# Three weight transfers asked for at other places of the start, one of them by another queue

## The chip, the cores and the metric

The kernel runs on one core of a Trainium2 chip. A core has five engines with an instruction stream each: TensorE (PE, matmuls and transposes), VectorE (DVE), ScalarE (ACT), GpSimd (POOL) and SyncE (SP), which only asks for DMA transfers. SP and ACT each have a DMA queue, and both queues are served by the same 16 DMA engines; in the profile, q1 is SP's queue and q10 is ACT's. The metric is the device time of one execution in microseconds, as the median of several executions; lower is better.

## The reference

Two stages follow each other. The first is an mLSTM cell with 4 batches, 8 heads, 768 steps and a head dimension of 40:

```python
for t in range(S):
    m_new = np.maximum(f_gate[:, :, t] + m, i_gate[:, :, t])
    f_stab, i_stab = np.exp(f_gate[:, :, t] + m - m_new), np.exp(i_gate[:, :, t] - m_new)
    C = f_stab * C + i_stab * outer(v_t, k_t)      # one 40x40 state for each batch and head
    n = f_stab * n + i_stab * k_t
    y[:, :, t] = sigmoid(o_gate_t) * (C @ q_t) / maximum(abs(n @ q_t), 1)
```

The second is a SwiGLU block on the 3072 tokens of width 320 that come out of it, with a hidden width of 1536:

```python
g = x @ w_gate
out = (g * sigmoid(g) * (x @ w_val)) @ w_out
```

The inputs of the first stage are float32. The three weight matrices arrive as float64, so the kernel reads them as pairs of 32-bit words and converts them to float32 itself.

## The kernel before

**Tiling.** The sequence is cut into six groups of 128 steps. For each group the kernel computes the cell's output in a chunked form (scores inside a chunk, a running state between chunks), turns it into `xT`, the transposed input of the second stage, and then runs the second stage on the group's 512 tokens. The hidden width is cut into 12 blocks of 128, m = 0 to 11. For group g, `hidden(g, m)` makes 20 matmuls (five chunks of 64 features, each for the gate and the value weights, and each matmul of float32 stands twice in the profile) into two PSUM banks, then ACT takes SiLU of the gate bank and DVE multiplies it with the value bank into `h_sb`. There are four such banks (`gen`), so block m needs the banks of block m - 2 back. After the blocks, `project` multiplies `h_sb` with the output weights `wo_sb`.

**Order.** The order of the instructions of each engine is the order in which the program text calls them (`manual_schedule`); no planner moves anything. Waits between engines come from the data that instructions share. A DMA transfer also takes one of eight DMA semaphores in turn and waits until the transfer that had it before has landed.

**Weights.** A piece is one or more blocks of weights, and is loaded by `piece_load(p)`: pieces 0 and 1 hold one block each (block 0, block 1), pieces 2 to 6 hold two blocks each (2 and 3, 4 and 5, 6 and 7, 8 and 9, 10 and 11), and pieces 7 to 9 hold the output weights. Pieces 0 to 6 come in two halves: the gate half, which goes to partitions 0 to 63, and the value half, which goes to partitions 64 to 127. A half is 320 KB for pieces 0 and 1 and 640 KB for the others. "The third piece" below is piece 2, "the fourth" piece 3, "the fifth" piece 4. The raw words land in the two buffers `raw` in turn, except for piece 2, which lands in a part of `h_sb` that is not used yet, and piece 3, which lands in `wo_sb`, also not used yet. The gate half is asked for by SP. Who asks for the value half is in one line:

```python
queues = (nc.sync, nc.scalar if p < 5 else nc.sync)
```

A block is then converted in three steps, `convert(j)`: `scale(j)` on ACT (`top`, then `low`, L190 and L192), `join(j)` on DVE (L199, L200) and `rounded(j)` on POOL or DVE (L207). In the first group the conversions of later blocks stand inside `hidden(0, m)`, ahead of the SiLU of that block: `hidden(0, 0)` converts block 2, `hidden(0, 1)` block 3, and so on.

**The start.** Everything around the change stands in the stretch before the first `hidden`: ACT loads the sigmoid's table and takes `sig(0)` and `sig(1)` of the output gates `o_sb` (heads 0 to 15 and 16 to 31, L463), then copies `xT`, scales block 0, copies `xT` again, scales block 1, takes the exp of `step1` (L609) and scales block 2. SP's stream asks in this stretch for the gate halves, then for the first group's `M_sb` to be written to `M_dram`, and then for what the second group (n = 1) needs: k and q (`load_all`, L117), piece 6, the attention weights `w_sb` from `M_dram` (`weights_load`, L447), v, the output weights and the output gates. `weights_sub` (L451) is the first to read `w_sb`, on DVE, and stands between the products of blocks 6 and 7 of the first group.

Of the kernel before, what the change touches and what calls it, by code (L numbers as in the profile page):

```python
# [12 lines left out]
U32 = mybir.dt.uint32  # L13
# [11 lines left out]
def kernel(  # L25
# [18 lines left out]
    nc = tc.nc  # L44
# [12 lines left out]
    NKC = DM // HP  # L57
    UH = BH // 2
    UA = UH // 2
    NH = NFC + 1  # L60
# [25 lines left out]
    def heads(P):  # L86
        return slice(P * UH, (P + 1) * UH)
# [13 lines left out]
    wo_sb = const.tile([128, NFC, DM], F32)  # L101
    h_sb = const.tile([128, NH, TW], F32)
# [34 lines left out]
    raws = {}  # L137
    PIECES = [("gv", 0, 1), ("gv", 1, 1)] + [("gv", m, 2) for m in range(2, NFC, 2)] + [("o", m, 4) for m in range(0, NFC, 4)]

    def piece_load(p, home=None):  # L140
        kind, m, n = PIECES[p]
        if kind == "gv":
            a, d = NKC, n * 128
            src = [(slice(i * HP, (i + 1) * HP), w[:, m * 128:(m + n) * 128].rearrange("(c p) f -> p c f", p=HP))
                   for i, w in enumerate((moe_w_gate, moe_w_val))]
            queues = (nc.sync, nc.scalar if p < 5 else nc.sync)
        else:
            a, d = n, DM
            src = [(slice(0, 128), moe_w_out[m * 128:(m + n) * 128].rearrange("(a p) d -> p a d", p=128))]
            queues = (nc.sync,)  # L150
        if src[0][1].dtype == F32:
            for r, w in src:
                if kind == "o":
                    nc.sync.dma_start(out=wo_sb[r, m:m + n, :], in_=w)
                else:
                    for x in range(n):
                        nc.sync.dma_start(out=wgv_sb[r, m + x], in_=w[:, :, ts(x, 128)])
            return
        if home is None:
            raw = conv.tile([128, 4 * NKC * 128], U32, name="raw")  # L160
        else:
            raw = home.rearrange("p a t -> p (a t)").bitcast(U32)
        raw = raw[:, 0:2 * a * d]
        for (r, w), queue in zip(src, queues):
            queue.dma_start(out=raw[r].rearrange("p (a d) -> p a d", a=a), in_=w.bitcast(U32))
        words = raw.rearrange("p (a d two) -> p a d two", two=2, a=a)
        raws[p] = (words[:, :, :, 0], words[:, :, :, 1])
        split(p)
# [4 lines left out]
    def split(p):  # L173
        if p in raws:
            lo, hi = raws.pop(p)
            kind, m, n = PIECES[p]
            if kind == "gv":
                for c in range(n):
                    r = slice(c * 128, (c + 1) * 128)
                    blocks[m + c] = (lo[:, :, r], hi[:, :, r], wgv_sb[:, m + c])  # L180
            else:
                for c in range(0, n, 2):
                    blocks[NFC + (m + c) // 2] = (lo[:, c:c + 2], hi[:, c:c + 2], wo_sb[:, m + c:m + c + 2, :])

    def scale(j):
        if j in blocks:
            lo, hi, dst = blocks[j]
            a, d = hi.shape[1], hi.shape[2]
            top = conv.tile([128, NKC * 128], F32, name="top", bufs=1).rearrange("p (a d) -> p a d", a=a)
            nc.scalar.mul(top, hi.bitcast(F32), 2.0 ** -112)  # L190
            low = conv.tile([128, NKC * 128], I32, name="low").rearrange("p (a d) -> p a d", a=a)
            nc.scalar.mul(low, lo, 2.0 ** -29)  # L192
            blocks[j] = (low, top.bitcast(U32), dst)

    def join(j):
        if j in blocks:
            lo, top, dst = blocks[j]
            both = dst.bitcast(U32)
            nc.vector.tensor_scalar(both, top, scalar1=3, scalar2=None, op0=ALU.logical_shift_left)  # L199
            nc.vector.scalar_tensor_tensor(both, in0=top, scalar=0x80000000, in1=both, op0=ALU.bitwise_and,  # L200
                                           op1=ALU.bitwise_or)
            blocks[j] = (lo, dst.bitcast(I32))

    def rounded(j, eng=None):
        if j in blocks:
            lo, dst = blocks.pop(j)
            (eng or nc.gpsimd).tensor_tensor(dst, dst, lo, op=ALU.add)  # L207

    def convert(j, eng=None):
        scale(j)  # L210
        join(j)
        rounded(j, eng)
# [34 lines left out]
    for u in range(B):  # L247
        r = slice(u * BH, (u + 1) * BH)
# [34 lines left out]
    def late_decay():  # L283
        nc.vector.tensor_add(m_in[:, 0:1], M0[0:BH, end].unsqueeze(1), f0[0:BH, end].unsqueeze(1))
        nc.vector.tensor_add(m_in[:, 1:], M_sb[:, 0:NL - 1, last], f_sb[:, 0:NL - 1, last])
        nc.vector.tensor_sub(step1, m_in.to_broadcast([BH, NL, SUB]), M_sb)
# [175 lines left out]
    def sig(P):  # L462
        nc.scalar.activation(o_sb[:, heads(P)], o_sb[:, heads(P)], AF.Sigmoid)  # L463


    def burn(n, tag="cell"):
        t = bank("burn", tag)
        for _ in range(n):
            nc.tensor.matmul(t, lhsT=junk[:, 0:128], rhs=junk, start=True, stop=True)
# [62 lines left out]
    def first_x(u):  # L532
        y = first_y.pop(u)
        den = work.tile([128, UH, 1], F32, name="den")[:, 0:H]
        nc.vector.tensor_scalar(den, y[:, :, D:], scalar1=1.0, scalar2=None, op0=ALU.max)
        nc.vector.scalar_tensor_tensor(den, in0=y[:, :, D:], scalar=-1.0, in1=den, op0=ALU.mult, op1=ALU.max)
        nc.vector.reciprocal(den, den)
        nc.vector.tensor_tensor(x_sb[:, u, 0:DM].rearrange("p (h d) -> p h d", d=D), y[:, :, 0:D],
                                den.to_broadcast([128, H, D]), op=ALU.mult)
# [39 lines left out]
    first_turn(1, q_sb, qT, (A, V))  # L579
    load(o_sb, o_gate, 0, 1)  # L580
    piece_load(0)
    piece_load(1)
    late_maxima()
    first_own(1)
    first_values(1)
    first_scores(1)
    first_x(1)
    sig(0)
    sig(1)
    piece_load(2, h_sb[:, NH - NKC:])  # L590
    piece_load(3, wo_sb)
    burn(3)
    first_own(2)
    first_own(3)
# [11 lines left out]
    first_state(0, A)  # L606
    late_decay()
    convert(1)
    nc.scalar.activation(step1, step1, AF.Exp)  # L609
    piece_load(5)  # L610
    nc.sync.dma_start(out=M_dram, in_=flat(M_sb))
# [234 lines left out]
```

## Time and profile before

| what | value |
|---|---|
| time, median of 3 runs | 555.15 us (554.77 to 555.56) |
| profiled execution: time | 555.16 us |
| profiled execution: span, first to last instruction | 553.0 us |
| TensorE busy | 546.4 us, 99% of the span |
| ScalarE busy | 134.7 us, 24% |
| VectorE busy | 234.4 us, 42% |
| q1 (SP): packets, MB | 222036, 42.11 |
| q10 (ACT): packets, MB | 1908, 2.85 |
| granted clock of TensorE | 1.000 |

The time of an execution is some 2 us longer than the span of its instructions. In the timeline, a row has its start in us, its busy time, the engine, the line, the operation, the output and the inputs, and in brackets how long the engine was idle before it and what ended that wait. Rows of SPq and ACTq are the instructions by which SP and ACT ask for transfers, and their time is that of the asking. In the chain of waits, a row with DMA runs from the asking to the landing.

### The profile page before, as it was taken

How to read it: one execution, taken by the hardware profiler on the slowest of the kernel's cores; microseconds unless marked ns; L12 is line 12 of the kernel's file. 1: busy time of each engine (PE TensorE's matmuls, PEld its weight loads, DVE VectorE, ACT ScalarE, POOL GpSimd, SP SyncE). 2: the span in 40 equal slices, each digit the busy share in tenths (PEclk: the TensorE clock that was granted, in tenths of full speed). 3: DMA queues.
4: the chain of work that ended last, by engine and by line, in shares of the span. 5: the costliest groups of instructions: out<-in, count | busy, mean ns of one | idle time of the engine just before them, and what ended most of it. 6: DMA issues, size and time to landing. Idle time of an engine off the chain costs nothing.

```text
span 553.0 us, 11595 instructions
## 1 busy us (share of the span) xinstructions
PE 546.4 (99%) x4992; PEld 312.9 (57%) x4992; DVE 234.4 (42%) x394; ACT 134.7 (24%) x202; POOL 106.6 (19%) x97
## 2 busy tenths in 40 slices
PE   8999999999999999999999999999999999999997
PEld 4955546675545575544576455466455567444475
DVE  5956687962156332445521445531426621011100
ACT  4366564443101033110124101005110100111100
POOL 2314355574011151011133001114001200000000
PEclk9999999999999999999999999999999999999999
DMA  9999996798631763660464451395000131000000
GB/s 125 177 280 187 192 274 115 155 111 125 68 49 17 108 109 83 71 76 5 82 127 104 53 68 27 49 149 107 13 1 2 29 62 43 12 1 0 2 24 24
DMA packets 223994, 45.69 MB, mean 83 GB/s; under 512 B 214504, under 2 KB 219112, under 8 KB 223944
## 3 DMA queue, kind: packets, MB, share of 16 engines
q1 hardware_dynamic: 222036, 42.11, 46.7%
q10 hardware_dynamic: 1908, 2.85, 2.0%
q8 instruction: 39, 0.64, 0.5%
q14 instruction: 11, 0.09, 0.1%
HBM read 35.68 MB, written 4.01 MB: 72 GB/s over the span
## 4 chain that ended last, share of the span: by engine, by line
PE 92%; DMA 4%; SPq 3%; POOL 0%; DVE 0%; ACT 0%; issue 0%; ACTq 0%; POOLq 0%
PE gv_ps L648 55%; PE o_ps L664 24%; PE o_ps L671 5%; SPq L117 3%; DMA h_sb<-in_moe_w_val_dram 2%; PE inter L377 2%; PE sp L331 2%; PE intra L382 2%; DMA o_sb<-in_o_gate_dram 2%; PE add L353 1%; PE tp_kq L296 0%; POOL wgv_sb L207 0%; PE tp_x L439 0%; DVE wgv_sb L200 0%; ACT top L190 0%
## 5 line engine op out<-in xcount | busy, mean ns | idle before, releaser
L648 PE MATMUL gv_ps<-xT,wgv_sb 64*128 64x512 f32 x1440 | 317.3, 593 | 1.6 <-POOL wgv_sb L207 1.1
L648 PEld LDWEIGHTS gv_ps<-xT,wgv_sb 64*128 64x128 f32 x1440 | 139.1, 187 | 159.4 <-issue 154.6
L654 DVE TENSOR_TENSOR h_sb<-sg,gv_ps 128x512 f32<-128x512 f32 x72 | 49.5, 687 | 214.5 <-ACT sg L653 214.4
L664 PE MATMUL o_ps<-wo_sb,h_sb 128*128 128x320 f32 x480 | 130.5, 433 | 0.0
L664 PEld LDWEIGHTS o_ps<-wo_sb,h_sb 128*128 128x128 f32 x480 | 90.8, 190 | 41.0 <-issue 3.8
L653 ACT ACTIVATE sg<-gv_ps 128x512 f32<-128x512 f32 x72 | 43.0, 597 | 268.6 <-PE gv_ps L648 268.5
L362 POOL TENSOR_TENSOR C<-C,dec 128x328 f32<-128x328 f32 x20 | 14.5, 735 | 137.7 <-DVE C L369 137.6
L456 POOL TENSOR_SCALAR_AFFINE_SELECT w_sb<-w_sb 64x1024 f32<-64x1024 f32 x20 | 27.8, 1388 | 60.2 <-DVE w_sb L451 59.3
L658 ACT COPY z_sb<-o_ps 128x320 f32<-128x320 f32 x24 | 10.0, 422 | 94.7 <-PE o_ps L664 90.9
L403 POOL TENSOR_TENSOR o_sb<-o_sb,y_sb 128x640 f32<-128x640 f32 x10 | 14.3, 1428 | 79.2 <-DVE y_sb L394 79.1
L671 PE MATMUL o_ps<-wo_sb,h_sb 128*128 128x320 f32 x96 | 26.9, 437 | 0.0
L451 DVE TENSOR_TENSOR w_sb<-g_T,w_sb 128x1024 f32<-128x1024 f32 x10 | 13.2, 1355 | 27.6 <-DMA w_sb<-M_dram 27.6
L426 DVE STREAM_TRANSPOSE xT<-x_sq 128x640 f32<-128x640 f32 x16 | 12.5, 822 | 23.7 <-DMA x_sq<-x_sb 23.7
L671 PEld LDWEIGHTS o_ps<-wo_sb,h_sb 128*128 128x128 f32 x96 | 17.9, 190 | 7.2
L394 DVE TENSOR_TENSOR y_sb<-y_sb,intra 64x328 f32<-64x328 f32 x40 | 19.7, 493 | 0.8 <-PE intra L382 0.2
L369 DVE TENSOR_TENSOR C<-C,add 40x328 f32<-40x328 f32 (+1 forms) x36 | 17.7, 493 | 1.3 <-PE add L353 0.4
L207 POOL TENSOR_TENSOR wgv_sb<-wgv_sb,low 128x640 int32<-128x640 int32 x8 | 12.3, 1541 | 23.7 <-DVE wgv_sb L200 21.9
L377 PEld LDWEIGHTS inter<-C,qT 64*64 64x64 f32 x640 | 10.2, 134 | 7.3 <-issue 6.1
L341 POOL TENSOR_TENSOR vw_sb<-v_sb,w_sb 128x656 f32<-128x656 f32 x10 | 12.8, 1303 | 0.4
L338 DVE TENSOR_TENSOR w_sb<-sp,w_sb 128x512 f32<-128x512 f32 x20 | 12.7, 682 | 0.0
L460 ACT ACTIVATE w_sb<-w_sb 128x1024 f32<-128x1024 f32 x10 | 10.6, 1058 | 8.8 <-POOL w_sb L456 8.8
L397 DVE TENSOR_SCALAR den<-den 128x16 f32<-128x16 f32 x10 | 12.2, 1216 | 0.3
(129 smaller groups left out, 343.7 us busy)
## 6 DMA issues: line engine op xcount, KB each, us to landing
w_sb<-M_dram SPq DMA_DIRECT2D x10, 512.0 KB, 7.2
x_sq<-x_sb SPq DMA_DIRECT2D x128, 40.0 KB, 2.0
k_sb<-in_k_dram SPq DMA_DIRECT2D x12, 320.0 KB, 6.1
v_sb<-in_v_dram SPq DMA_DIRECT2D x12, 320.0 KB, 5.7
o_sb<-in_o_gate_dram SPq DMA_DIRECT2D x12, 320.0 KB, 5.4
raw<-in_moe_w_out_dram SPq DMA_DIRECT2D x3, 1280.0 KB, 7.8
out_dram<-z_sb SPq DMA_DIRECT2D x24, 160.0 KB, 1.8
q_sb<-in_q_dram SPq DMA_DIRECT2D x32, 64.0 KB, 2.4
```

The lines of the kernel that those rows point to most:

```text
L117: nc.sync.dma_start(out=dst[:, heads(P), 0:D], in_=tokens(a, c, P))
L362: nc.gpsimd.tensor_tensor(state(s + 1)[:, a], state(s)[:, a], dec[:, s - 2, a].unsqueeze(2).to_broadcast([128, UA, D1]), op=ALU.mult)
L369: nc.vector.tensor_tensor(c, c, ps[r], op=ALU.add)
L377: nc.tensor.matmul(inter[two][half(i), a, :], lhsT=qT[half(two), P * UA + a, half(i)], rhs=state(2 * n + i)[half(two), P * UA + a, :], sta ...
L394: nc.vector.tensor_tensor(t, t, intra[i][half(c)], op=ALU.add)
L403: eng.tensor_tensor(o, o, y[:, :, 0:D], op=ALU.mult)
L456: nc.gpsimd.affine_select(w, w, compare_op=ALU.is_ge, fill=NEG, base=0, pattern=[[0, UH], [1, SUB]], channel_multiplier=-1)
L648: nc.tensor.matmul(ps[i], lhsT=wgv_sb[half(i), m, PAIRS[kc][i] if g < 2 else kc, :], rhs=x[half(i), kc, :], start=(kc == 0), stop=(kc == N ...
L653: nc.scalar.activation(sg, ps[0], AF.Silu)
L654: nc.vector.tensor_tensor(hid(g, m), sg, ps[1], op=ALU.mult)
L664: nc.tensor.matmul(p, lhsT=hid(g, m)[:, ts(u, L)], rhs=wo_sb[:, m, :], start=(m == 0), stop=(m == NFC - 1))
L671: nc.tensor.matmul(ps[u], lhsT=hid(g, m)[:, ts(u, L)], rhs=wo_sb[:, m, :], start=(m == 0), stop=(m == NFC - 1))
```

## The change

The asking for the two halves of a piece is taken apart. `piece_load` asks for the gate half at once, and keeps the asking for the value half in `asks`; with `later=True` it leaves it there, and `value_half(p)` does it. Three things move with that:

- Piece 2 (the third) is asked for between `sig(0)` and `sig(1)`. SP's part of it keeps its place in SP's stream; on ACT the value half now stands ahead of `sig(1)` where it stood behind it.
- Piece 3 (the fourth) has its gate half asked for at the same place as before. Its value half, still asked for by ACT, stands behind `convert(1)`, that is behind ACT's scaling of block 1, and ahead of the exp of `step1`.
- Piece 4 (the fifth) has its value half asked for by SP, behind its gate half, where ACT asked for it ahead of the second part of `first_seam(1, ...)`.

The number of transfers, their sizes and where they land stay the same. All other instructions keep their order on each engine.

```diff
+    asks = {}
+
+    def value_half(p):
+        for ask in asks.pop(p, ()):
+            ask()
+
-    def piece_load(p, home=None):
+    def piece_load(p, home=None, later=False):
...
-            queues = (nc.sync, nc.scalar if p < 5 else nc.sync)
+            queues = (nc.sync, nc.scalar if p < 4 else nc.sync)
...
-        for (r, w), queue in zip(src, queues):
-            queue.dma_start(out=raw[r].rearrange("p (a d) -> p a d", a=a), in_=w.bitcast(U32))
+        asks[p] = [lambda r=r, w=w, queue=queue: queue.dma_start(out=raw[r].rearrange("p (a d) -> p a d", a=a), in_=w.bitcast(U32))
+                   for (r, w), queue in zip(src, queues)]
+        asks[p].pop(0)()
+        if not later:
+            value_half(p)
...
     sig(0)
+    piece_load(2, h_sb[:, NH - NKC:])
+    piece_load(3, wo_sb, later=True)
     sig(1)
-    piece_load(2, h_sb[:, NH - NKC:])
-    piece_load(3, wo_sb)
     burn(3)
...
     convert(1)
+    value_half(3)
     nc.scalar.activation(step1, step1, AF.Exp)
     piece_load(5)
```

## The prediction

> **What bounds the kernel now.** I read the page first, then the chain of waits, then TensorE's, ScalarE's and VectorE's timelines of the first 90 us, then what each DMA queue moved there.
>
> ```profile
> PE 546.4 (99%) x4992; PEld 312.9 (57%) x4992; DVE 234.4 (42%) x394; ACT 134.7 (24%) x202; POOL 106.6 (19%) x97
> ...
> DMA  9999996798631763660464451395000131000000
> ...
> q1 hardware_dynamic: 222036, 42.11, 46.7%
> q10 hardware_dynamic: 1908, 2.85, 2.0%
> ```
>
> TensorE is busy for 546.4 of 553.0 us, so nothing but its idle 6.6 us can be won. The DMA engines are full in slices 0 to 5 (up to 83 us) and slack later: an early transfer that comes later has no free time to catch up in before then. q1 holds what SP asks for, q10 what ACT asks for. In the chain, one piece of the changed region stands out:
>
> ```profile
> 25.43 13.59 DMA h_sb<-in_moe_w_val_dram
> ...
> 39.17 0.81 ACT top L190
> ...
> 41.51 1.54 POOL wgv_sb L207
> 43.05 0.04 issue
> 43.10 4.80 PE gv_ps L648 x20
> ```
>
> The third piece's value half is asked for at 25.43, lands at 39.02, and ACT, DVE and POOL then convert block 2 (39.17 to 43.05), for which TensorE waits:
>
> ```profile
> 37.45 4.56 PE L648 MATMUL gv_ps<-xT,wgv_sb 64*128 64x512 f32 x20
> 43.10 4.80 PE L648 MATMUL gv_ps<-xT,wgv_sb 64*128 64x512 f32 x20 [1.08 <-POOL wgv_sb L207]
> ...
> 68.54 13.10 PE L648 MATMUL gv_ps<-xT,wgv_sb 64*128 64x512 f32 x60
> ```
>
> The gap of 1.08 us (0.2% of the time) is all that the move can remove there. From 43.10 to the last row TensorE has no gap. That row is three blocks of 4.37 us (7, 8, 9), so block 9 starts at 68.54 + 8.73 = 77.27.
>
> The second place to look at is VectorE before block 9:
>
> ```profile
> 70.97 1.22 DVE L451 TENSOR_TENSOR w_sb<-g_T,w_sb 128x1024 f32<-128x1024 f32 x1 [1.31 <-DMA w_sb<-M_dram]
> ...
> 75.87 0.68 DVE L654 TENSOR_TENSOR h_sb<-sg,gv_ps 128x512 f32<-128x512 f32 x1
> ```
>
> VectorE waits 1.31 us for the attention weights' DMA, is then busy without a break, and ends the product of block 7 at 76.55. Block 9 needs the two PSUM banks that this product frees (four banks, two a block). So between that DMA and TensorE there is a slack of only 77.27 - 76.55 = 0.72 us.
>
> **What the Trainium skill says.** (1) "SBUF — State Buffer", section "Door 1: The DMA port swizzle": 64 partitions reach 8 of the 16 ports, measured 196 GB/s. The trace agrees: gate halves go to partitions 0 to 63, value halves to 64 to 127, and from 25 to 32 us q1 alone moves 1.38 MB in 7 us, 197 GB/s:
>
> ```profile
> DMA packets 1026, 1.40 MB, mean 200 GB/s; under 512 B 48, under 2 KB 646, under 8 KB 1025
> ...
> q1 hardware_dynamic: 1011, 1.38, 109.1%
> q10 hardware_dynamic: 14, 0.01, 0.9%
> ```
>
> (2) The same page, "Can I just issue two DMAs to hit both halves?", says no, 6% at most. Here the trace differs, and it decides: from 36.5 to 43.5 us, with gate halves on q1 and value halves on q10, the two move 353 GB/s, 1.23 and 1.24 MB:
>
> ```profile
> q10 hardware_dynamic: 629, 1.24, 53.4%
> q1 hardware_dynamic: 631, 1.23, 51.8%
> ```
>
> So q1 makes 197 GB/s alone and 176 with q10 beside it. (3) "DMA: Bandwidth & Descriptors", "Issuing engines are not separate DMA queues", says the asking engine saves only issue time. For halves of the partitions, (2) says otherwise.
>
> **The change, part by part.** ScalarE now:
>
> ```profile
> 21.58 0.74 ACT L463 ACTIVATE o_sb<-o_sb 128x640 f32<-128x640 f32 x1
> 25.42 0.74 ACT L463 ACTIVATE o_sb<-o_sb 128x640 f32<-128x640 f32 x1 [3.11 <-DMA o_sb<-in_o_gate_dram]
> 25.43 0.60 ACTq L165 DMA_DIRECT2D h_sb<-in_moe_w_val_dram  x1
> 26.07 0.63 ACTq L165 DMA_DIRECT2D wo_sb<-in_moe_w_val_dram  x1
> ...
> 30.04 0.61 ACTq L165 DMA_DIRECT2D raw<-in_moe_w_val_dram  x1
> ```
>
> *Third piece's value half.* It now follows the second sigmoid, which waits for its gate data. Between the sigmoids it is asked for at about 21.6, 3.8 us earlier and ahead of SP's gate halves for pieces 2 and 3 (22.94, 23.69). Today q10 moves 0.01 MB from 25 to 32 us: the request stands behind SP's. Earlier, it should run from about 25 beside q1, 0.655 MB at 177 GB/s = 3.7 us, and land at 29 to 32. ACT is free for it at 35.5 (the exp at 34.78 + 0.74). Block 2 must begin to be scaled by 42.01 - 3.93 = 38.1 for TensorE to run on, so the 1.08 us go even if it lands 6 us later than I say. The 0.60 us of issue lie inside ACT's wait of 3.11 us: cost nothing; were that wait gone, 0.6 us beside 0.88 us of slack before the copies at 27.04.
>
> *What it takes from piece 0.* Scaling block 0 waits 0.39 us for its gate half (ACT at 28.50), and from there ACT and DVE run unbroken to block 0's first matmul at 31.90. q1 slowed from 197 to 176 GB/s between 25 and 28.4 costs 3.4 x 0.12 = 0.4 us; bounds 0 (not beside it yet) and 2 (half of the 3.7 us, if the value half goes in front). I take 0.3. TensorE is then early by 1.08 - 0.3 = 0.78 us at block 2.
>
> *Fourth piece's value half,* from 26.07 to about 32.7, behind the scaling of block 1. Behind it on ACT are a table load, the exp and block 2's scaling, which are not needed before 38.1; ACT then was idle for 3.66 us, which covers the 0.63. It lands between 40 and 46. Block 4's conversion takes 4.87 us (45.05 on ACT to 49.92 on POOL) and its matmuls start at 53.52, 0.8 us earlier afterwards, so it may begin at 52.7 - 4.9 = 47.8. Cost nothing, with 2 us of cover in the late case; beyond that, TensorE waits at block 4 for as long as it is later.
>
> *Fifth piece's value half by SP.* ACT loses an issue of 0.61 us at 30.04, so its copies at 30.69 come earlier; block 0 waits as much for DVE (31.76), so this gains nothing. SP gains a 0.6 us issue, and it waits for piece 1's gate half (30.17), whose semaphore it takes over in the built program. Behind it on SP stand piece 5, M_dram, k, q, piece 6 and w_sb. SP's issues are early (k waits from 39.5 to 50.1 in a full queue), so only the data count: q1 carries 0.655 MB more before all of these.
>
> *How late q1 becomes.* Today q1 needs from 25.0 to about 46.8 (21.8 us) for 3.93 MB. Afterwards 4.59 MB: the two value halves left on q10 (1.31 MB) run 7.4 us beside it, in which q1 moves 1.30 MB; 3.29 MB at 197 GB/s take 16.7 us; 24.1 us. Gate and value halves in turn on q1 go a little faster (205 GB/s from 58 to 63.5 us), 0.4 us less. So 1.9 us late. From 49.2 to 50.4 DMA moves only 27 GB/s (SP's second k transfer is held up); a later queue can swallow 1.0 us of this hole. Bounds for w_sb: 0.9 and 1.9 us late, taken 1.2.
>
> *What this does.* w_sb late by d moves block 7's product to 76.55 + d, and block 9 to 76.60 + d against 77.27: the sum is d - 0.67, or -0.78 where that is less. With d = 1.2: +0.5 us. TensorE's early start is spent waiting for banks, so the 0.3 above does not matter. Later stages follow TensorE: DMA has empty time from 98.6 to 101.6.
>
> The profiled execution took 555.16 us for its span of 553.0; the median is 555.15, so the sum stands on either: 555.6.
>
> **The rivals.** *A, the queue's delay is absorbed* (d under 0.3): the hole at 49.2 and better mixing of halves on q1 take it up. For it: the hole is real. Against: 0.655 MB at 197 GB/s is 3.3 us. Then -0.7 us: 554.5. *B, slower: w_sb's delay in full.* Place: VectorE's wait at 70.97. From d = 0.7 it costs, from 1.8 it passes 0.2%. If, besides, the fourth value half runs while the fifth's is on q1, both write the upper 64 partitions and share 197 GB/s: 3.7 us beside the third's half (0.65 MB), then 3.94 + 0.66 MB at 197 GB/s, 23.3 us, make 27.0 us, 5.2 over today's 21.8; less 0.4 and 1.0 as above d = 3.8, so +3.1 us, 558.3. For it: today the third value half stood behind SP's requests just so. Price +1.2 to +3.1. *C, faster:* gap gone, piece 0 not slowed, w_sb not late, and block 2's 0.24 us over a normal block also gone: -1.3, 553.9. Against: it needs w_sb earlier by 0.6. *D, the ask at 21.6 brings nothing* and the gap stays: block 9 then still waits for w_sb, so the total is that of the main case or B.
>
> **How the numbers follow.** Main case (d 0.7 to 1.8, D included) 0.45, A 0.17, B 0.30, C 0.08. A measurement of this kernel tells about 0.2%, 1.1 us. Main and A lie within: same 0.62; B 0.30 slower; C 0.08 faster. The range goes from A's -0.9 to +2.1 in B, leaving out C and B's upper third: 554.2 to 557.3.
>
> **What would show it.** q10 1908 packets to about 1570 and 2.2 MB. Block 2's gap of 1.08 gone, its value half landed before 35. VectorE's wait at L451 for w_sb longer than 1.31 us and ending at 71.9 to 72.9, and a new TensorE gap of 1 to 2 us near 76.5, ended by VectorE's L654. If that wait ends at 71 and TensorE has no gap there, A or C holds; if it ends after 73, B. A gap elsewhere before 60 us makes my steps wrong.

## The result and the profile after

The changed kernel takes **560.72 us** (median of 13 runs, 557.34 to 564.09) against 555.3 us before (13 runs beside them, 554.71 to 557.62). The ratio is 1.009, with a 95% interval of 1.0065 to 1.0114: it is slower by 0.65 to 1.1%. I had predicted 555.6, at most 557.3. The profiled execution took 562.75 us for a span of 560.6, so it is 2.0 us longer than the median, and what follows from its trace adds up to that time, not to the median. Ratios and intervals here leave out executions that are over 1.5% longer than the quickest of the same kernel; below there are two, of 562.17 and of 565.29 us.

The page of the changed kernel first: busy time, share and count for TensorE, the DMA engines' busy tenths in 40 slices of the span, and the two queues with packets, MB and share.

```profile
PE 548.4 (98%) x4992; PEld 317.4 (57%) x4992; DVE 233.2 (42%) x394; ACT 134.7 (24%) x202; POOL 106.4 (19%) x97
...
DMA  9999998598641395353285353295000131000000
...
q1 hardware_dynamic: 222372, 42.77, 48.0%
q10 hardware_dynamic: 1572, 2.20, 2.1%
```

One value half of 0.65 MB has gone from q10 to q1, as the diff says. TensorE's busy time has grown by 2.0 us, and its idle time from 6.6 to 12.2 us. TensorE's timeline shows both:

```profile
30.05 1.13 PE L561 MATMUL add<-vw_sb,k_sb 128*64 128x41 f32 x32
35.15 6.16 PE L658 MATMUL gv_ps<-xT,wgv_sb 64*128 64x512 f32 x20 [3.96 <-DVE m_in L294]
...
42.30 8.85 PE L658 MATMUL gv_ps<-xT,wgv_sb 64*128 64x512 f32 x40
...
84.38 4.56 PE L658 MATMUL gv_ps<-xT,wgv_sb 64*128 64x512 f32 x18 [2.92 <-DVE h_sb L664]
```

Block 0 starts at 35.15 (before 31.90) after a gap of 3.96 us, and takes 6.16 us instead of 4.56. The gap before block 2 is gone: the row at 42.30 is blocks 1 and 2 in one. A new gap of 2.92 us stands in block 9, behind its first two matmuls, ended by VectorE's product. The chain of waits names what is behind the two gaps; a DMA row runs from the asking to the landing:

```profile
19.31 12.38 DMA raw<-in_moe_w_gate_dram
35.15 6.16 PE gv_ps L658 x20
...
64.50 14.23 DMA w_sb<-M_dram
80.41 1.65 DVE wgv_sb L209
84.38 4.56 PE gv_ps L658 x18
```

**The first place** is the landing of piece 0's gate half, asked for at 19.31. ScalarE's timeline, with its request for the third piece's value half, and SP's below it:

```profile
21.59 0.74 ACT L472 ACTIVATE o_sb<-o_sb 128x640 f32<-128x640 f32 x1
21.59 0.60 ACTq L170 DMA_DIRECT2D h_sb<-in_moe_w_val_dram  x1
...
31.77 0.77 ACT L199 ACTIVATE top<-raw 128x640 f32<-128x640 f32 x1 [3.84 <-DMA raw<-in_moe_w_gate_dram]
```

```profile
19.31 3.83 SPq L170 DMA_DIRECT2D raw<-in_moe_w_gate_dram  x2
23.18 0.62 SPq L170 DMA_DIRECT2D h_sb<-in_moe_w_gate_dram  x1
```

SP's row joins two issues, the gate halves of pieces 0 and 1. By the trace's single instructions the first lasts from 19.31 to 22.26: SP is held in it. ScalarE's request for the third value half is out at 22.20, ahead of it by 0.06 us. The queues from 25.4 to 28.4 us then read:

```profile
q10 hardware_dynamic: 276, 0.53, 93.8%
q1 hardware_dynamic: 66, 0.07, 12.4%
```

In the kernel before, q1 had 0.59 MB and q10 0.01 in the same 3 us. So the third value half is served first, nearly alone, and lands at 29.93; piece 0's gate half follows and lands at 31.69, where it landed at 28.42 before.

**The second place** is VectorE's wait for `w_sb`:

```profile
78.75 1.23 DVE L460 TENSOR_TENSOR w_sb<-g_T,w_sb 128x1024 f32<-128x1024 f32 x1 [5.83 <-DMA w_sb<-M_dram]
...
83.65 0.68 DVE L664 TENSOR_TENSOR h_sb<-sg,gv_ps 128x512 f32<-128x512 f32 x1
```

It ends at 78.75 instead of 70.97. The product of block 7 stands behind it and is done at 84.33; block 9 goes on at 84.38. q1 is late because of the front and because of what happens from 41.5 to 47.5 us, when the fifth value half runs on q1 and the fourth on q10 (by a count of q1's bytes, the gate half ahead of it has been moved by 41.9 us, though its last part lands at 45.42):

```profile
DMA packets 610, 1.22 MB, mean 204 GB/s; under 512 B 12, under 2 KB 12, under 8 KB 610
...
q10 hardware_dynamic: 302, 0.62, 55.3%
q1 hardware_dynamic: 308, 0.61, 51.5%
```

Both queues are busy, and together they move 204 GB/s. Before, with gate halves on one queue and value halves on the other, the two moved 353 GB/s. The two value halves share their 64 partitions, and also the matrix that they are read from; no run separates these two.

So the 7.6 us between the two spans are made of two pieces. Up to block 8, TensorE is 3.25 us late (76.14 against 72.89): 3.25 by block 0's start, 1.60 by block 0's length, less 1.25 and 0.35 at blocks 1 to 3, where the old gap was. From the start of block 9 to that of block 10 it needs 10.46 us instead of 6.41, that is 4.05 more. The remaining 0.3 us lie later.

### The profile page after: what moved, and what is told of

Same layout as the page of the kernel before. It is cut to its first block, busy times and chain, and to the rows that moved or that the text cites. A ratio compares the mean times of both kernels' runs of the same rounds, so it can differ in the third digit from the quotient of the medians.

```text
span 560.6 us, 11597 instructions
## 1 busy us (share of the span) xinstructions
PE 548.4 (98%) x4992; PEld 317.4 (57%) x4992; DVE 233.2 (42%) x394; ACT 134.7 (24%) x202; POOL 106.4 (19%) x97
## 4 chain that ended last, share of the span: by engine, by line
PE 89%; DMA 5%; SPq 4%; DVE 1%; ACT 1%; issue 0%; ACTq 0%
PE gv_ps L658 53%; PE o_ps L674 23%; PE o_ps L681 5%; SPq L117 3%; DMA w_sb<-M_dram 3%; DMA raw<-in_moe_w_gate_dram 2%; PE inter L386 2%; PE sp L340 2%; PE intra L391 2%; PE add L362 1%; DVE wgv_sb L209 0%; PE tp_x L448 0%; DVE h_sb L664 0%; DVE w_sb L460 0%; SPq L170 0%
## 5 line engine op out<-in xcount | busy, mean ns | idle before, releaser
L658 PEld LDWEIGHTS gv_ps<-xT,wgv_sb 64*128 64x128 f32 x1440 | 143.5, 188 | 162.7 <-issue 151.4
L199 ACT ACTIVATE top<-raw 128x640 f32<-128x640 f32 x12 | 9.6, 798 | 11.6 <-issue 5.5
```

The costliest lines, as they stand in the source:

```text
L658: nc.tensor.matmul(ps[i], lhsT=wgv_sb[half(i), m, PAIRS[kc][i] if g < 2 else kc, :], rhs=x[half(i), kc, :], start=(kc == 0), stop=(kc == N ...
```

## The experiments

The theory after this reading: **(1) front**, the early request overtakes SP's first gate half in the service and delays block 0; **(2) block 9**, `w_sb` comes later than TensorE's block 9 can bear, from the fifth's 0.65 MB on q1 and from the fourth and fifth value halves writing the same 64 partitions at once. Against these stand rivals that are named in the expectations. Differences below are of medians, each against the kernel before in the same comparison (554.95 to 555.3 us).

### Each part of the change alone

The third piece alone (the request between the sigmoids; pieces 3 and 4 as before):

```diff
     sig(0)
+    piece_load(2, h_sb[:, NH - NKC:])
     sig(1)
-    piece_load(2, h_sb[:, NH - NKC:])
     piece_load(3, wo_sb)
```

> Only the first part: the third piece's value half between the sigmoids; fourth and fifth as before. Theory FRONT (ACT's early request is served before SP's first gate half, alone, so block 0 and all of q1 come some 3.3 us later): block 0's first matmul at about 35 instead of 31.9, the 1.08 us gap at block 2 gone, w_sb about 3 us late, sum +2 to +3 us (557.5 to 558.5). Theory LOAD (the delay comes from the fifth value half on SP's queue): block 0 at 32, sum -0.7 us (554.5).

Measured: 555.74 us (12 runs, 553.45 to 562.17), ratio 1.001 (0.9985 to 1.0035). Its profiled execution was the longest of the twelve. There the request went out at 22.77 and piece 0's gate half landed at 34.96, so that block 0 waited still longer than in the changed kernel:

```profile
38.42 6.76 PE L657 MATMUL gv_ps<-xT,wgv_sb 64*128 64x512 f32 x20 [5.67 <-DVE m_in L294]
```

The median, though, hardly moves: the delay cannot be there in every run. I therefore ran the same kernel again, to see one of its commoner executions.

> The same kernel as third_only, for a profile of one of its common executions. Theory FRONT-BY-CHANCE: ACT's request and SP's first gate half are set free by the same landing of o_sb, and who comes first differs from run to run; then a common, quick execution has block 0 at about 32 and no gap at block 2, and the times lie in two groups, near 554.5 and at 558 to 562. Theory FRONT-ALWAYS: block 0 is at 34.5 or later in it too, and the quick time comes from elsewhere.

Measured: 556.0 us (16 runs, 552.98 to 559.78), ratio 1.002 (1.0001 to 1.0039). The profiled execution took 554.45 us. SP's and TensorE's timelines in it:

```profile
19.13 2.03 SPq L170 DMA_DIRECT2D raw<-in_moe_w_gate_dram  x2
```

```profile
33.34 4.56 PE L657 MATMUL gv_ps<-xT,wgv_sb 64*128 64x512 f32 x20 [0.28 <-DVE m_in L294]
```

Here SP was held less long: its first gate half was out at 20.50 and ScalarE asked only at 20.82. Piece 0's gate half landed at 27.42, the third value half after both first gate halves, at 33.34, and block 0 had no gap of note. It still starts 1.44 us later than before, because TensorE was slower ahead of it, at a granted clock of 0.76 from 24 to 31 us.

So the front delay is the outcome of a race. In the five traces with the early request, ScalarE asks 0.02 to 0.03 us after the first `o_sb` transfer has landed (at 21.57 in the changed kernel). SP's first gate half is out 0.69 to 1.06 us after that landing in the three with the delay, and 0.29 and 0.38 us ahead of it in the two without. What lets SP go no run shows. The single trace of the first run had shown one side only.

The fourth piece alone (its value half behind `convert(1)`):

```diff
-    piece_load(3, wo_sb)
+    piece_load(3, wo_sb, later=True)
...
     convert(1)
+    value_half(3)
```

> Only the second part: the fourth piece's value half behind the scaling of block 1. FRONT and LOAD both expect no change, 555.2 within 0.6 us: q10 stands idle or full as before, and block 4 isn't needed before 47. Theory SHARE (late fourth and fifth value halves run at once into the upper 64 partitions) also expects none here, as both are then on ACT's queue one after the other.

Measured: 555.39 us (20 runs), ratio 0.9999 (0.9988 to 1.0011). The half landed at 46.97 and no matmul waited for it. By itself this part costs nothing.

The fifth piece alone:

```diff
-            queues = (nc.sync, nc.scalar if p < 5 else nc.sync)
+            queues = (nc.sync, nc.scalar if p < 4 else nc.sync)
```

> Only the third part: the fifth piece's value half asked for by SP. LOAD: q1 is 1.9 to 3.3 us later, the wait of VectorE for w_sb ends at 73 to 74 instead of 70.97, a TensorE gap of 1 to 3 us before block 9, sum +1.2 to +2.6 us (556.4 to 557.8). FRONT: 555.2, no gap.

Measured: 557.73 us (20 runs), ratio 1.0036 (1.002 to 1.0052), +2.4 us. VectorE and TensorE at block 9:

```profile
72.04 1.23 DVE L451 TENSOR_TENSOR w_sb<-g_T,w_sb 128x1024 f32<-128x1024 f32 x1 [3.14 <-DMA w_sb<-M_dram]
```

```profile
77.67 4.56 PE L648 MATMUL gv_ps<-xT,wgv_sb 64*128 64x512 f32 x18 [0.24 <-DVE h_sb L654]
```

This is the place and the releaser that the prediction named. Only the wait is not yet as long as in the changed kernel: from the start of block 9 to that of block 10 TensorE needs 1.36 us more than before. That is not the whole loss. This execution's span is 2.06 us longer than before, and up to block 11 TensorE is only 0.59 us late. Another 1.15 us come between the starts of blocks 11 and 12, where TensorE stands still among matmuls of one group:

```profile
102.72 0.67 PE L382 MATMUL intra<-v_sb,w_sb 64*64 64x41 f32 x30 [1.45 <-issue]
```

The profile names nothing that ends this stop. It comes at the same matmul in seven of the fourteen traces, 0.18 to 1.45 us long, 0.33 us in the first trace of the kernel before and 0.88 us in that of the fourth part alone, which costs nothing. In all seven TensorE goes on 1.2 to 1.6 us after a packet of q8, the queue for instructions, has ended, so a late fetch of instructions is likely, but not shown. How much of the median's 2.4 us is the wait at block 9 therefore stays open.

### Parts together

The third and the fourth piece, the fifth's value half still by ScalarE (the changed kernel with `p < 5`):

> The whole change but for the fifth value half, which ACT asks for as before. FRONT: block 0 at about 35, w_sb 3 us late, +2 to +3 us (557.5 to 558.5). LOAD or SHARE as the sole cause: the loss is gone, 554.5 to 555.5. If the three parts add up, the rest to the changed kernel (560.7) is what the fifth costs when the other two are there.

Measured: 557.96 us (20 runs, 556.0 to 561.22), ratio 1.0045 (1.003 to 1.006), +2.7 us. The trace has the front, and no wait at block 9:

```profile
34.47 6.26 PE L658 MATMUL gv_ps<-xT,wgv_sb 64*128 64x512 f32 x20 [3.05 <-DVE m_in L294]
```

ScalarE asked at 20.96; SP's first gate half was out at 21.81 and landed at 31.01. Block 9 starts 2.67 us late, and block 10 follows 6.42 us later, as before the change. Between blocks 11 and 12 another 1.05 us are lost, with the stop described above:

```profile
104.71 0.67 PE L391 MATMUL intra<-v_sb,w_sb 64*64 64x41 f32 x30 [1.39 <-issue]
```

Why this pair loses more in the median than the third piece alone is not settled. None of its 20 times lies under 556.0 us, where 10 of the 28 of the third piece alone lie under 555. It may lose the race more often or lose elsewhere; no trace shows one of its quickest executions.

The fourth and the fifth piece, the third as before (the diff is against the changed kernel):

```diff
     sig(0)
-    piece_load(2, h_sb[:, NH - NKC:])
-    piece_load(3, wo_sb, later=True)
     sig(1)
+    piece_load(2, h_sb[:, NH - NKC:])
+    piece_load(3, wo_sb, later=True)
```

> The second and third parts of the change together, the third's value half asked for where the kernel before asks for it. LOAD (the fifth's value half costs SP's queue its time, whatever the fourth's does): as the fifth part alone, 557.7 (557.2 to 558.3), the wait of VectorE for w_sb at 3 us. SHARE (the fourth's and the fifth's value halves write the upper 64 partitions side by side at half the pace, so that they cost more together than each by itself): 559 to 561, the wait 5 us or more, and a TensorE gap of 2 us or more before block 9.

Measured: 559.45 us (5 runs, 558.42 to 562.27), ratio 1.0079 (1.0064 to 1.0093), +4.5 us. The fourth alone costs 0.1 and the fifth alone 2.4, so some 2 us come only when both are there. Its timelines at block 9:

```profile
77.82 1.23 DVE L460 TENSOR_TENSOR w_sb<-g_T,w_sb 128x1024 f32<-128x1024 f32 x1 [5.50 <-DMA w_sb<-M_dram]
```

```profile
83.44 6.01 PE L658 MATMUL gv_ps<-xT,wgv_sb 64*128 64x512 f32 x18 [2.60 <-DVE h_sb L664]
```

The profiled execution was the longest of the five and had a late front too: the second `o_sb` transfer landed at 27.45, and TensorE waited 2.96 us before block 0, without any early request. So a late front can come by chance as well. The waits of this trace are not typical; the interaction rests on the five times.

### The front taken out

Third piece alone, but with the request held back for 2 us on ScalarE by a copy of one element that VectorE writes at 23.5 us. It then stands behind SP's first gate halves, but is still some 2 us earlier than before the change:

```diff
     sig(0)
+    nc.scalar.copy(warm[0:1], W0[0:1, UH + 1, 0:1])
+    piece_load(2, h_sb[:, NH - NKC:])
     sig(1)
-    piece_load(2, h_sb[:, NH - NKC:])
     piece_load(3, wo_sb)
```

> The third piece's value half between the sigmoids, but ACT first copies one element that VectorE writes at about 22.7, so that it is asked for at about 23, behind SP's first two gate halves (until 22.9) instead of just ahead of them. Theory FRONT (transfers are served in the order in which they are asked for, one queue standing while the other's is ahead): block 0 back at 31.9 to 32.4 without a TensorE gap of 3 us, value half landed before 35, gap at block 2 gone, sum -0.5 to -0.9 us (554.3 to 554.8). Rival MIX (the value half takes bandwidth from the gate halves wherever it stands): block 0 still 2 us late or more, 557 to 558.

Measured: 555.16 us (14 runs), ratio 1.0004 (0.9986 to 1.0022). Block 0 starts at 33.65 with a gap of 0.28 us, and the third value half, asked for at 23.48, lands at 36.77, early enough for block 2, which has no gap. So in the traces it is the place ahead of the gate half that delays block 0, not the request being early; the times of the third piece alone and of this version do not differ beyond their intervals. Nor is this version faster than the kernel before, though it keeps the hoped-for effect. Its block 0 is late for another reason: piece 0's gate half landed at 27.57, ahead of the 28.42 of before, but TensorE was busy until just before block 0, at a clock of 0.76 (the last figures of this row of stretches are the granted clock, the DMA share and GB/s):

```profile
24.00:31.00 7.00, 7.00 (x45) 5.79 (x44) 5.87 (x20) 3.27 (x5) 0.73 (x2) 0.76 1.12 203
```

The mean clock on record is 0.997 or less in 12 of its 14 executions, and in 23 of the 47 of the kernel before beside them. Whether the early request brings this about, and what it costs in the median, no run shows.

The same copy in the changed kernel, all three parts in place:

```diff
     sig(0)
+    nc.scalar.copy(warm[0:1], W0[0:1, UH + 1, 0:1])
     piece_load(2, h_sb[:, NH - NKC:])
```

> The changed kernel with all three requests moved as in the change, but the third piece's value half asked for about 2 us later: ScalarE first copies one element that VectorE writes at about 23.5 us, which is after SP's first gate half is out (20.4 to 22.3). FRONT (the 2.7 us of the first part come from the third's value half being served ahead of the first gate half; the rest, some 2.5 us, is the fifth's on SP's queue): no TensorE gap before block 0, block 0 by 34, and about 557.8 (557.2 to 558.4). ORDER-FREE (it is the mere bringing forward of the third, with more transfers under way in the first 50 us, that costs): 560 or more.

Measured: 558.8 us (5 runs, 557.68 to 559.43), ratio 1.007 (1.0057 to 1.0082), +3.9 us. There is no gap before block 0, which starts at 33.88. My expectation put 557.8, with the fifth's cost alone left. It is 1 us more; the fourth and fifth value halves overlap here too: the fifth's landed 5.13 us after the gate half ahead of it on q1 (41.83 to 46.96), where it needed 3.09 us in the fifth part alone (42.20 to 45.29).

```profile
74.03 1.23 DVE L460 TENSOR_TENSOR w_sb<-g_T,w_sb 128x1024 f32<-128x1024 f32 x1 [3.98 <-DMA w_sb<-M_dram]
```

```profile
79.66 4.55 PE L659 MATMUL gv_ps<-xT,wgv_sb 64*128 64x512 f32 x18 [1.08 <-DVE h_sb L665]
```

The interval of this ratio and that of the changed kernel (1.0065 to 1.0114) overlap. That the gap before block 0 is gone is shown by the trace; that it was worth 1.6 us rests on the medians alone.

### The wait at block 9 taken out

The changed kernel, with the first two uses of the second group's `w_sb` one block later, so that block 7's product no longer stands behind them on VectorE:

```diff
-        6: [run(turn, 1, (A, A), (A, V)), run(weights_sub, 1, 0), run(weights_mask, 0), run(piece_load, 7)],
-        7: [run(weights_sub, 1, 1), run(weights_mask, 1), run(nc.gpsimd.memset, q_sb, 0.0)],
+        6: [run(turn, 1, (A, A), (A, V)), run(piece_load, 7)],
+        7: [run(weights_sub, 1, 0), run(weights_mask, 0), run(weights_sub, 1, 1), run(weights_mask, 1), run(nc.gpsimd.memset, q_sb, 0.0)],
```

> The changed kernel, but the first reading of w_sb on VectorE (weights_sub and weights_mask of the lower heads) stands behind the product of block 7 instead of ahead of it. Theory PATH (late w_sb holds that product, and so block 9's banks): the TensorE gap of 2.9 us before block 9 is gone, block 0's delay stays, sum 557.5 to 558.2. Rival ELSEWHERE (another late transfer, q or piece 6, takes its place at once): 560 to 561.

Measured: 556.57 us (12 runs, 553.75 to 565.29), ratio 1.0018 (0.9998 to 1.0037), +1.6 us, or +0.9 without the one execution at 565.29. The same transfers, the same sizes and queues; only VectorE's order is other, and 3.8 of the 5.4 us are gone (4.5 without that execution). Its runs still fall apart: five at 553.75 to 554.91 and five at 557.28 to 558.2, with one between and one beyond. The profiled execution is the quickest; SP had its first gate half out at 20.04 there, ahead of ScalarE's request at 20.45.

Both remedies at once (the copy and the later `w_sb`):

> The changed kernel with the third's value half asked for 2 us later (behind SP's first gate half) and with the w_sb sums of head 1 moved one block later, so that the delay of w_sb no longer stands ahead of block 7's product on VectorE. TWO CAUSES (the front and the wait at block 9 are the whole loss): 555.0 (554.4 to 555.7), no TensorE gap over 0.4 us after block 0. A THIRD CAUSE: 556.5 or more.

Measured: 555.4 us (21 runs, 554.19 to 558.64), ratio 1.0013 (1.0001 to 1.0024), +0.45 us. Blocks 0 to 9 run without a gap over 0.3 us. Behind block 10, `w_sb` is still late for the additions, and the stretch from block 10 to block 11 takes 8.18 us, where it took 6.50 before the change, though the gaps in it look small:

```profile
82.03 5.16 PE L659 MATMUL gv_ps<-xT,wgv_sb 64*128 64x512 f32 x20
87.36 0.31 PE L362 MATMUL add<-vw_sb,k_sb 64*64 64x41 f32 x2 [0.17 <-DVE w_sb L347]
87.95 2.33 PE L362 MATMUL add<-vw_sb,k_sb 64*64 64x41 f32 x126 [0.29 <-DVE w_sb L347]
90.21 4.56 PE L659 MATMUL gv_ps<-xT,wgv_sb 64*128 64x512 f32 x20
```

So part of the wait has only moved. In the median, the two remedies together take back the loss but for 0.13% (0.01 to 0.24%). The two taken one at a time give back 1.6 us (front) and 3.8 us (block 9).

### Was there anything to gain?

The kernel before once more, for a second trace of it:

> The kernel before once more, for a second profile. If the 1.08 us TensorE gap before block 2 belongs to the kernel, it is there again (0.8 to 1.3 us), and what the change takes away there is worth about 1 us in each run. If it belonged to that one execution (the fourth part alone, which does not move what block 2 waits for, had 0.17 us there, and the fifth part alone none), it is under 0.5 us, and the change had nothing to gain.

Measured: 554.93 us (10 runs). TensorE:

```profile
32.63 4.56 PE L648 MATMUL gv_ps<-xT,wgv_sb 64*128 64x512 f32 x20 [1.36 <-DVE m_in L285]
...
43.45 4.81 PE L648 MATMUL gv_ps<-xT,wgv_sb 64*128 64x512 f32 x20 [0.70 <-POOL wgv_sb L207]
```

The gap is there, with the same releaser, but 0.70 us long, between the two cases of the expectation. In the run with the fourth part alone, which asks for the third piece where the kernel before does, it was 0.17 us, and with the fifth part alone there was none. It varies with the landing that starts the request (25.43 in the first trace with 1.08 us of gap, 26.10 here, 24.89 with the 0.17, 22.88 with none) and with block 0, which here starts 0.73 us later itself.

The gap can also be taken away without touching a transfer, by rounding block 2 on VectorE:

```diff
-        first = [run(convert, j, V if j in on_vector else None) for j in ahead[m]]
+        first = [run(convert, j, V if j in on_vector or j == 2 else None) for j in ahead[m]]
```

> The kernel before, with only the last step of block 2's conversion on VectorE (0.82 us) instead of GpSimd (1.53 us). No transfer moves. If the gap of 1.08 us is all that block 2 costs, it shrinks to about 0.3 us and the time falls by 0.7 to 0.8 us, 554.5; if VectorE is then late for block 0's product, no change.

Measured: 555.32 us (14 runs), ratio 1.0011 (0.9997 to 1.0025). The gap is gone:

```profile
37.21 9.34 PE L648 MATMUL gv_ps<-xT,wgv_sb 64*128 64x512 f32 x40
```

and the median is not better, though this profiled execution, at 553.79 us, was the quickest of the fourteen. Two versions without the gap in their traces, then, and neither gains: the intervals leave room for 0.14% (0.8 us) in the one and 0.03% (0.2 us) in the other. No version came out faster than the kernel before.

## Why the prediction was wrong, step by step

Two steps failed, the cost of the early request to piece 0 ("I take 0.3") and d, the lateness of q1. By the medians d is the larger: with the wait at block 9 taken out 3.8 of the 5.4 us are gone, with the front taken out 1.6.

**The gap before block 2: right in the trace, wrong in worth.** The gap went and the value half landed at 29.93, inside the 29 to 32. But "beside q1 ... at 177 GB/s" failed: it ran in front of q1. And a gap of one execution was taken for a gain of every execution; four traces of unmoved third requests have 1.08, 0.70, 0.17 and 0 us.

**"I take 0.3": the first step that failed.** The upper bound, 2 us, was for half of the value half going in front; in the changed kernel's trace the whole of it did, and piece 0's gate half came 3.27 us later. The evidence had been in the trace that I quoted: before, the third request waited behind SP's for 7 us without moving more than 0.01 MB. I read there that a queue waits for what was asked ahead of it, and then let q1 run on when the order was turned round. The Trainium skill ("DMA: Bandwidth & Descriptors", section "Queues, rings and completion order") says that the DMA engines take turns between the queues, packet by packet. From 41.5 to 47.5 us the trace agrees, with 0.62 and 0.61 MB; from 25.4 to 28.4 it does not, with 0.53 and 0.07, and there the measurement decides. A mechanism for the order is not shown by any run; that the order of asking matters is, by the traces of the third piece alone and of the two versions with the copy.

**What the clock added.** Block 0 after the gap took 6.16 us, 1.60 more than before, at a granted clock of 0.73 from 35.15 to 41.2. The Trainium skill ("TensorE: Matmul & The Clock Gate", section "What's actually happening") has the clock halved after an idle window of some 3.4 us, with windows that run freely, and so a loss of about half a window, 1.7 us by estimate. The traces agree roughly: gaps of 3.96, 3.05 and 5.67 us were each followed by a block 0 of 6.16 to 6.76 us, and a gap of 2.60 us once by 6.01 us for 18 matmuls that otherwise take 4.56. The clock of the changed kernel's block 0 is the 0.73 in this row:

```profile
35.15:41.20 6.05, 6.05 (x20) 2.63 (x20) 3.53 (x5) 5.40 (x7) 2.44 (x2) 0.73 1.07 198
```

But 3.05 and 2.60 us are less than the window that the page names, and the 2.92 us before the rest of block 9 were followed by 4.56 us, without a loss. Nor is a gap the only cause: the third piece alone had, in its second run and with the copy, a clock of 0.76 from 24 to 31 us with no gap near it. The prediction had no term for this.

**"The 0.3 above does not matter": failed too.** It holds only if block 9's wait is fixed while TensorE moves. Here the front moved TensorE and q1 together, by 3.25 and at first 3.3 us, so the front came on top of block 9's loss rather than inside it.

**The fourth's half at no cost: right alone, wrong beside the fifth.** It was priced by what TensorE needs of it (block 4), and not by what it does to the other queue.

**d, the lateness of q1: the second step that failed.** Taken 1.2 (0.9 to 1.9), against a TensorE that stays in place. Measured against the start of block 9, the end of VectorE's wait moved by 1.84 us with the fifth alone (from 6.21 us ahead to 4.37), inside my bounds; by 2.68 with all three parts and the copy; by 4.53 in the changed kernel. So with the fifth alone d was in range; it failed where the fourth's value half had been moved as well. The terms: the fifth's value half took 3.09 us of q1 alone, 4.78 in the changed kernel (landing 45.42 to 50.20) where it shared the upper partitions with the fourth's, while I had let q1 run at 176 GB/s beside two value halves for 7.4 us. The hole at 49.2 us, which I let swallow 1.0 us, swallowed nothing in the changed kernel: piece 5's gate half came 7.31 us late, k 7.37, `w_sb` 7.78. With the fifth alone it did: 2.30 us late ahead of it, 1.31 behind.

**The slack at block 9: right but for 0.2 us.** I had 0.67 us. The stretch from block 9 to block 10 grew by 1.36, 2.20 and 4.05 us for the three shifts of 1.84, 2.68 and 4.53: each time 0.48 us less than the shift. With the third and fourth parts alone, where the shift is -0.31, it grew by 0.01. With the fourth and fifth it grew by 5.18 for a shift of 4.21, that is 3.73 by the same rule and 1.45 by the slower 18 matmuls. The place, the releaser and the formula held; what was fed into it did not.

**The rivals.** B had the mechanism of the second place, with d = 3.8 and 558.3 us; the changed kernel without the front gave 558.8. That the totals are so near is in part luck, as the trace of that version has 2.68 for d. B had 0.30, as the main case let both value halves left on q10 run beside q1. None of the rivals had the front. The text did say that a gap elsewhere before 60 us would make the steps wrong, and it is there, at block 0.

## What to carry to other kernels

Before bringing a transfer forward, ask what it will then stand in front of: price the other queue's first transfer as late by the whole of what may now go ahead of it, and look for who waits for that. When transfers that each fill half of the partitions are moved between queues, see which halves meet: here a lower and an upper half together gave 353 GB/s (in the kernel before), two upper ones 204 (in the changed one). And take a gap's worth from several traces; one of 0.2% of the time may be the chance of one execution.

## What the runs showed of the hardware

- Two queues, each filling its own 64 partitions, make 353 GB/s together; one such transfer alone makes 196 to 200, and two queues into the same 64 partitions, both reading one matrix, 204.
- A request on ScalarE's queue, out 0.06 us ahead of SP's, was served for 3 us almost alone. SP's request for piece 0 is held for 1.4 to 4.2 us in its issue, and in the five traces with the early request this decides who is first. It may be a reason why the times of the changed kernel spread more (557.3 to 564.1 us, against 554.7 to 557.6 before); only for the third piece alone are there traces of both sides, at 562.17 and 554.45 us.
- Block 0 after a TensorE gap of 3.0 to 5.7 us took 1.6 to 2.2 us longer than its 4.56 us, at a granted clock of 0.73 in the changed kernel. The clock also fell to 0.76 from 24 to 31 us in two traces where TensorE had had no gap over 0.2 us since 14 us.
- TensorE stopped for 0.18 to 1.45 us at one and the same matmul near 100 us in seven of fourteen traces, with no wait that the profile names; each time it went on 1.2 to 1.6 us after a packet of the instruction queue had ended.
